# The second group's q and k as Strassen quads, v stores on GpSimd's queue, and later loads of v weights, in a fused attention and gated-MLP kernel

## The chip, the cores and the metric

One Trainium2 chip, one core. The metric is the device time of the whole kernel in microseconds (us); a version's time is the median of its runs.

## The reference: what is computed

The input x has 2048 tokens of 1024 features, in bf16. Two branches are computed from it and mixed by a gate per token:

```python
g = sigmoid((x * gate_w).sum(-1, keepdims=True))
a = A(x, wqkv, wo)       # 32 heads of 32; each token attends to 8 tokens, 2 apart, at or before it
b = B(x, w_in, w_sp, b_sp, w_out)
return g * a + (1 - g) * b
```

A is `x @ wqkv`, split into q, k and v, a softmax over the eight logits of a token and head, the weighted sum of eight v rows, and a product with `wo`. B is a gelu of `x @ w_in`, whose second half is normalised per token and mixed over all tokens with the 2048x2048 matrix `w_sp`; the product of the two halves goes through `w_out`.

## The kernel before, in words

TensorE works through these stages: a start that loads x transposed (15 transposing DMAs), makes v for the first twelve heads and q, k of group 0; then the q and k of the other seven groups of four heads, with v of the other heads and a part of z2 between; then z2, z1, the spatial product and the output product. The attention itself runs on VectorE, group after group, beside TensorE's products.

**Names.** `xT` is x transposed, tokens in the columns; `xts` holds four sums of its quarters, made by `x_sums` (line 412), eight VectorE operations of 128x2048 elements. A *tile* (`qk_tile`, line 289) is a product of q or k of one group with 512 tokens: eight matmuls of 512 columns. A *quad* is the Strassen-Winograd form of a two-by-two block product: seven products instead of eight. `qk_quad(g, c, side)` (line 895) makes q and k of group g for 1024 tokens: its first block row is q, its second is k, its block columns are tokens at 512 c and at 1024 + 512 c. It needs `xts` and four weight sums (`qk_sums`, line 881), and uses the generator `chain` (line 498), which yields after each of its seven products, of four matmuls each. Between the products lie a seed copy from bank to bank on ScalarE (L517), a copy of the shared product into SBUF on ScalarE (L523), two additions `plus` in PSUM on VectorE (L505), and four copies of the results on ScalarE (L902). One quad has four banks of its own (`bank_roles`).

**Which groups are quads.** `PAIRS = (2, 4)`: groups 2 and 3, and groups 4 and 5, are quads. Groups 0, 1, 6 and 7 are tiles. The first tile of group 1 is played at the end of the start (line 402), the other seven in the list of `group_tiles(0)` (line 943). `play_group` (line 928) plays the quads: one among the matmuls of a group's bands (`among_bands`), two interleaved.

**Bands and attention.** Logits come as bands: `band_blocks` (line 337) multiplies q and k of a group for blocks of tokens into banks 4 to 7 (L355), ScalarE casts them to fp16 (L360, L363), and they are stored to `band_d`. From there `load_bands` (line 649) gathers each token's eight logits into `att_L`. On VectorE follow maxima (L670 to L673), on ScalarE the exponential (L661), on VectorE the sum, the reciprocal and the weights (L682 to L691), and the products with v and their sums (L707, L711, L712, L716). v goes through `v_d` in DRAM too. `vp_tile` (line 298) makes v of 128 tokens for the first three groups and the gate's logit; after every fourth tile three stores of 128 KB go out (line 310), 12 in all. `load_v` (line 636) reads a group's v back, 960 KB. v of the other five groups comes from eight `v_quad`s (line 598), played in group 2, with weights `wvr` (two loads of 640 KB) and four sums of them, `wvs`.

**What sets the order.** In the start each engine's instructions stand as they are written. From line 1000 a planner runs while the program is written: it keeps a clock for each engine, one for the DMA queue, and lists of what is due (`dma`, `fill`, and three streams of attention work: maxima, weights, products). After each product of TensorE, `step` calls `advance`, which places on VectorE, ScalarE and SyncE whatever the clocks say is ready by then. The order so found is fixed in the program: an engine whose next instruction waits does nothing else. The planner starts with figures for its clocks and for the bands and v (`T_START`, line 860, and line 1007). Nearly all DMAs are issued from SyncE's queue, in that order.

**Around the change, in time.** The start ends with v tiles 12 to 15 (39.3 to 43.4 us), the first tile of group 1, and the gate: a small matmul (L405), a tanh (L406), two VectorE operations, and the stores of g and 1 - g to DRAM. Behind these in the queue are the gather of group 0's bands, the load of g as attention reads it, the load of group 0's v, group 3's weights, and group 1's v. Then the seven tiles, and from 57.5 the first quad of group 2, with group 1's bands between its products.

Of the kernel before, what the change touches and what calls it, by code (L numbers as in the profile page):

```python
# [58 lines left out]
def kernel(  # L59
# [104 lines left out]
    def load_wqk(g, dma):  # L164
        for t in range(2):
            dma(wqk_slots[g][:, t], wq_v[:, :, t * D + g * C:t * D + (g + 1) * C])
# [118 lines left out]
    def low_bank():  # L285
        half_bank[0] += 1
        return banks[half_bank[0] % 4]
# [10 lines left out]
    def vp_tile(i, bank=None, middle=None):  # L298
        ps = bank() if bank else banks[i % 2]
        for kt in range(KT):  # L300
            if kt == (2 if i else 6) and middle is not None:
                middle()
            nc.tensor.matmul(ps[:, 0:VP + 1], xT[:, kt, i * P:(i + 1) * P], wvp[:, kt, :], start=(kt == 0), stop=(kt == KT - 1))  # L303
        st = vp_slots[i // 4]
        nc.scalar.copy(st[:, i % 4, :].rearrange("p (g d h) -> p g d h", g=GP, h=HG), ps[:, 0:VP].rearrange("p (g h d) -> p g d h", g=GP, h=HG))
        nc.scalar.copy(gl_s[:, i:i + 1], ps[:, VP:VP + 1])
        if i % 4 == 3:
            for g in range(GP):
                dv = bass.AP(tensor=v_d.tensor, offset=v_d.offset + (g * (S + 16) + 16 + (i - 3) * P) * C, ap=[[C, P], [P * C, 4], [1, C]])
                sync.dma_start(dv, st[:, :, g * C:(g + 1) * C])  # L310

    warm = reg(XS_OFF, 512)
    nc.vector.memset(warm, 0.0)
# [66 lines left out]
    def first_bands(c):  # L380
        band_blocks(0, *((0, 8, 2), (1, 1, 6, 3), (4, 1, 4, 2), (6, 1, 4, 2))[c])

    for c in range(4):
        tiles = range(4 * c, 4 * c + 4) if c else ()
        for n, i in enumerate(tiles if c < 3 else ()):
            vp_tile(i, low_bank)
            if n == 0:
                first_bands(c - 1)
        if c == 1:
            for m in range(2):  # L390
                sync.dma_start(wvr[m], wq_v[:, :, 2 * D + VP + VH * m:2 * D + VP + VH * (m + 1)])
        if c == 2:
            load_wqk(2, sync.dma_start)
        for t in range(2):
            qk_tile(0, t, c)
            if c == 3 and t == 0:
                first_bands(2)
    for i in tiles:
        vp_tile(i, low_bank)
        if i == 12:  # L400
            first_bands(3)
    qk_tile(1, 0, 0)

    glT = low_bank()[0:16, 0:P]
    gate_mm = nc.tensor.matmul(glT, gl_s[:], ident32[:], start=True, stop=True)  # L405
    gate_act = nc.scalar.activation(omg[:], glT, ACT.Tanh, scale=0.5)  # L406
    nc.vector.tensor_scalar(g_s[:], omg[:], 0.5, 0.5, ALU.mult, ALU.add)
    gate_vec = nc.vector.tensor_scalar(omg_h[:], omg[:], -0.5, 0.5, ALU.mult, ALU.add)
    sync.dma_start(bass.AP(tensor=g_d.tensor, offset=g_d.offset, ap=[[P, 16], [1, P]]), g_s[:])
    gate_dma = sync.dma_start(bass.AP(tensor=og_d.tensor, offset=og_d.offset, ap=[[P, 16], [1, P]]), omg_h[:])  # L410

    def x_sums(r):
        for c in range(2):
            lo, hi = slice(512 * c, 512 * c + 512), slice(1024 + 512 * c, 1536 + 512 * c)
            a, b = ((xT[:, 0:4, hi], xT[:, 0:4, lo]), (xT[:, 4:8, hi], xts[0][:, :, lo]),
                    (xT[:, 4:8, hi], xT[:, 0:4, hi]), (xT[:, 4:8, lo], xts[1][:, :, lo]))[r]
            nc.vector.tensor_tensor(xts[r][:, :, lo], a, b, ALU.subtract)  # L417

    for r in range(4):
        x_sums(r)  # L420

    quad = [0]
    bank_roles = [banks[0:4], banks[4:8]]
# [74 lines left out]
    def chain(A11, A12, A22, S1, S2, S3, S4, B11, B21, B22, T1, T2, T3, T4, vs, put, share, N, flip=False, side=None, lean=False, done=None):  # L498

        def pairs(a, b):  # L500
            return list(zip(b, a)) if flip else list(zip(a, b))

        def plus(out, a):
            dve(N / 960.0 + 0.14, clock["PE"] + 0.2)
            last_add[0] = nc.vector.tensor_tensor(out[:, n], a[:, n], vs, ALU.add)  # L505
            return last_add[0]

        side = quad[0] % 2 if side is None else side
        X, Y, Z, V = bank_roles[side]
        bank_roles[side] = [X, V, Y, Z] if lean else [Y, V, X, Z]  # L510
        quad[0] += 1
        n = slice(0, N)
        dur, copy = N / 600.0 + 0.01, N / 1400.0 + 0.22
        pe(dur)
        product(X, pairs(A11, B11), True, N)
        act(copy, clock["PE"] + 0.2)
        last_seed[0] = nc.scalar.copy(Y[:, n], X[:, n])  # L517
        yield
        pe(dur)
        product(V, pairs(S1, T1), True, N)  # L520
        (act if share == nc.scalar.copy else dve)(copy, clock["PE"] + 0.2)
        with tc.high_priority():
            share(vs, V[:, n])  # L523
        yield
        pe(dur)
        product(Y, pairs(S2, T2), False, N)
        with tc.high_priority():
            plus(Z, Y)
        yield
        pe(dur)  # L530
        product(X, pairs(A12, B21), False, N)
        with tc.high_priority():
            put(0, 0, X)
        yield
        pe(dur)
        product(Y, pairs(S3, T3), False, N)
        if not lean:
            act(copy, clock["PE"] + 0.2)
            seed = nc.scalar.copy(X[:, n], Y[:, n])
        with tc.high_priority():  # L540
            inst = plus(V, Y)
            if not lean:
                tc.add_manual_dep(inst.ins, seed.ins.name, SYNC, reason="one reader of a bank at a time")
            put(1, 1, V)
        yield
        pe(dur)
        product(Z, pairs(S4, B22), False, N)
        with tc.high_priority():
            put(0, 1, Z)
        yield  # L550
        pe(dur)
        W = Y if lean else X
        product(W, pairs(A22, T4), False, N)
        with tc.high_priority():
            put(1, 0, W)
        if done is not None:
            done()
        yield
# [298 lines left out]
    SQH = 8  # L857
    squares = [(n, x) for n in range(16) for x in range(2)]
    LEAN = (True, True)
    T_START = (0.5, 0.0, 2.5)  # L860

    def square(n, x, junk):
        c = slice(x * HF, (x + 1) * HF)
# [4 lines left out]
            junk = junk[:, c]  # L868
        return nc.scalar.activation(junk, src, ACT.Square, accum_out=(s2, s2h)[x][:, n:n + 1])  # L869

    sums4(wvs, wvr[0][:, 0:4], wvr[0][:, 4:8], wvr[1][:, 0:4], wvr[1][:, 4:8])

    NQ = (0, 0, 0, 0, 0, 0, 0, 0)
    quads = [(0, i) for i in range(7)] + [(1, i) for i in range(8)]

    QSET = [g + x for g in PAIRS for x in range(2)]
    qs_slots = [z2h[:, 0:16, 256 + 896 * r:384 + 896 * r].rearrange("p (q k) c -> p q k c", q=4) for r in range(2)]
    qv_slots = [reg(R_OFF + 34752 + 1024 * r, 1024).bitcast(F32) for r in range(2)]
    q_landed, q_free = {}, [int(2 in PAIRS), 0]

    def qk_sums(g):
        w, s = wqk_slots[g], qs_slots[g % 2]
# [43 lines left out]
        next(quad, 0)  # L926

    def play_group(g):
        if g + 1 in PAIRS:
            among_bands(g, qk_quad(g + 1, 0, 0))  # L930
            first = qk_quad(g + 1, 1, 0)
            for _ in range(2):
                next(first)
                step()
            mark(bank_roles[1][1:3], 512)
            run(qk_quad(g + 2, 0, 1), first, step=step)
        elif g in PAIRS:
            among_bands(g, qk_quad(g + 1, 1, 0))
        else:
            return False  # L940
        return True

    def group_tiles(g):
        if g + 1 < NG:
            tiles = [lambda t=t, c=c: qk_tile(g + 1, t, c) for t in range(2) for c in range(4)][not g:]
        else:
            tiles = [lambda a=a, m=m: z2_tile(7, a, m) for m in range(2) for a in range(2)]
        if g == 0:
            return tiles

        def band(x):
            band_set(g, x)
            if x == 2:
                bands_have[0] = g + 1
        band = [lambda x=x, f=band: f(x) for x in range(3)]
        if g - 1 in PAIRS:
            return tiles[0:2] + [tiles[2], band[0], tiles[3], band[1], tiles[4], tiles[5], band[2]] + tiles[6:]
        if g + 1 < NG:
            return [tiles[0], band[0], tiles[1], band[1], tiles[2], tiles[3], band[2]] + tiles[4:]
        return [tiles[0], band[1], tiles[1], band[0], tiles[2], band[2], tiles[3]]  # L960
# [36 lines left out]
    def load_wqk_later(g, at):  # L997
        dma(at, 2.9, lambda: load_wqk(g, sync.dma_start), (lambda t: qk_ready(g, t)) if g in QSET else None)

    settle()  # L1000
    live[0] = True
    for inst in (gate_mm, gate_act, gate_vec, gate_dma):
# [1 line left out]
    for x in clock:  # L1004
        clock[x] = 0.0
    band_data[0], band_free[0], v_data[0] = T_START
    clock["SP"], clock["DMA"] = 5.5, 5.5
    stored.clear()
    bands_have[0] = 1
    next_bands()  # L1010
    dma(0.0, 0.1, lambda: sync.dma_start(g_att[:], bass.AP(tensor=g_d.tensor, offset=g_d.offset, ap=[[NJ, P], [1, NJ]])))
    next_v(1)
    load_wqk_later(3, 0.0)
    next_v()
    if 2 in PAIRS:
        fill.extend((1.5, 0.34, f) for f in qk_sums(2))
    for g in range(NG):
# [634 lines left out]
```

## Time and profile before

| | us |
|---|---|
| median of 5 runs | 653.93 |
| lowest, highest run | 652.51, 655.25 |
| the profiled execution | 654.89 |
| its span (first to last instruction) | 653.1 |
| TensorE busy in the span | 643.7 |
| VectorE busy | 515.3 |
| ScalarE busy | 295.2 |
| GpSimd (POOL) busy, 15 instructions | 6.2 |

The profile is one execution. Its page has the busy time of each engine (PE is TensorE's matmuls, PEld its weight loads, DVE VectorE, ACT ScalarE, POOL GpSimd, SP SyncE; SPq is SyncE's DMA queue), the span in 40 slices, the DMA queues, the chain that ended last, and the costliest groups of instructions. Beside the page the trace answers questions: who waited for whom, and the instructions of one engine in order of time. There a row is the start in us, the time from the start of the first to the end of the last instruction of a run of like ones, engine, line, operation, tiles and shapes, the count, and in brackets the idle time before it and who ended it. The durations of like instructions next to each other overlap a little, and a matmul's end is modelled, so starts are a better measure than ends.

The sixteen DMA engines are most busy in the start (0.85 to 1.19 of their time by tens of us from 0 to 50, where over one means that packets overlap). The granted TensorE clock is 1.00 in every slice that was asked for, from 0 to 653 us.

### The profile page before, as it was taken

To read this page: it belongs to the slowest core of one execution; us is meant where nothing else is said; L and a number is where in the kernel's file an instruction comes from. 1 tells how busy PE (TensorE), PEld (TensorE's weight loads), DVE (VectorE), ACT (ScalarE), POOL (GpSimd) and SP (SyncE) were. 2 spreads that over 40 slices of the span, in tenths; PEclk is the share of its full clock that TensorE was granted. 3 is DMA by queue.
4 is the path that set the end of the run, shared out by engine and by line. 5 is a ranking of instruction groups with operands and counts; after the bars stand their busy time and mean duration, and the time that the engine had idled before them with its cause. 6 is when DMAs were issued, how large, how long until landed. Compare 5 with 4: busy or idle time off the path is not lost.

```text
span 653.1 us, 11331 instructions
## 1 busy us (share of the span) xinstructions
PE 643.7 (99%) x4399; PEld 337.2 (52%) x4399; DVE 515.3 (79%) x808; ACT 295.2 (45%) x640; POOL 6.2 (1%) x15
## 2 busy tenths in 40 slices
PE   8999999999999999999999999999999999999998
PEld 4544467544445555444444444444444444868684
DVE  0434989999799999999988676987659999686862
ACT  3445677766677777799644112111121112202020
POOL 1000000000000000001000000000000000000000
PEclk9999999999999999999999999999999999999999
DMA  9998755697768103247995577559487364555501
GB/s 196 188 220 208 151 115 145 145 233 177 166 181 216 23 6 121 64 129 198 290 222 189 108 172 176 130 167 282 117 184 169 97 136 107 121 137 124 119 31 52
DMA packets 232934, 98.19 MB, mean 150 GB/s; under 512 B 180640, under 2 KB 220208, under 8 KB 232880
## 3 DMA queue, kind: packets, MB, share of 16 engines
q1 hardware_dynamic: 232592, 97.27, 61.5%
q8 instruction: 34, 0.56, 0.4%
q10 hardware_dynamic: 288, 0.20, 0.1%
q14 instruction: 20, 0.16, 0.1%
HBM read 44.31 MB, written 36.61 MB: 124 GB/s over the span
## 4 chain that ended last, share of the span: by engine, by line
PE 75%; DVE 8%; ACT 6%; SPq 5%; DMA 4%; issue 2%; DVEq 0%; ACTq 0%
PE psum_all L434 58%; PE psum_all L1476 8%; PE psum_all L293 5%; SPq L194 3%; PE psum_all L303 2%; ACT arena L869 2%; SPq L189 2%; ACT arena L1167 1%; DVE psum_all L505 1%; DMA band_d<-arena 1%; DVE arena L707 1%; DMA arena<-in_A_wqkv_dram 1%; PE psum_all L355 1%; SPq L178 1%; DMA arena<-in_B_w_sp_dram 1%
## 5 line engine op out<-in xcount | busy, mean ns | idle before, releaser
L434 PE MATMUL psum_all<-arena 128*128 128x512 f16 (+6 forms) x2462 | 493.3, 362 | 3.0 <-ACT psum_all L517 1.4
L434 PEld LDWEIGHTS <-arena 128*128 128x128 f16 (+1 forms) x2462 | 239.7, 98 | 249.1 <-issue 5.3
L707 DVE TENSOR_TENSOR arena<-arena,att_A 128x2048 f16<-128x2048 bf16 x64 | 75.3, 1218 | 0.3
L293 PE MATMUL psum_all<-arena 128*128 128x512 bf16 x256 | 57.5, 379 | 0.2 <-DMA arena<-in_A_wqkv_dram 0.2
L505 DVE TENSOR_TENSOR psum_all<-psum_all,arena 128x512 f32<-128x512 f32 (+1 forms) x74 | 48.2, 667 | 7.4 <-PE psum_all L434 3.7
L1476 PE MATMUL psum_all<-arena 128*128 128x256 f16 (+1 forms) x468 | 52.0, 273 | 0.2 <-ACT psum_all L1482 0.2
L1476 PEld LDWEIGHTS <-arena 128*128 128x128 f16 x468 | 45.8, 98 | 6.1 <-issue 0.3
L814 ACT ACTIVATE arena<-psum_all 128x448 bf16<-128x448 f32 x64 | 34.2, 545 | 19.3 <-PE psum_all L434 9.0
L452 ACT COPY psum_all<-psum_all 128x512 f32<-128x512 f32 (+1 forms) x24 | 12.5, 520 | 66.9 <-PE psum_all L434 60.9
L1167 ACT ACTIVATE arena<-psum_all 128x512 bf16<-128x512 f32 x56 | 31.2, 614 | 21.1 <-DMA z_d<-arena 8.0
L293 PEld LDWEIGHTS <-arena 128*128 128x128 bf16 x256 | 24.3, 98 | 28.9 <-DMA arena<-in_A_wqkv_dram 0.6
L711 DVE TENSOR_TENSOR arena<-arena 128x2048 f16<-128x2048 f16 x32 | 38.0, 1217 | 0.0
L363 ACT CAST arena<-psum_all 128x1988 f16<-128x1988 f32 (+3 forms) x25 | 34.0, 1359 | 2.4 <-PE psum_all L355 2.0
L296 ACT CAST arena<-psum_all 128x512 bf16<-128x512 f32 x32 | 18.6, 585 | 27.2 <-PE psum_all L293 27.2
L869 ACT ACTIVATE arena<-arena 128x896 bf16<-128x896 bf16 x32 | 30.9, 980 | 0.0
L476 ACT COPY psum_all<-psum_all 128x512 f32<-128x512 f32 (+1 forms) x24 | 12.3, 518 | 37.5 <-PE psum_all L434 36.8
L576 DVE TENSOR_TENSOR arena<-arena 128x512 f16<-128x512 bf16 (+3 forms) x52 | 25.4, 521 | 2.3 <-DMA arena<-in_A_wqkv_dram 1.9
L417 DVE TENSOR_TENSOR arena<-arena 128x2048 f16<-128x2048 bf16 x8 | 9.4, 1222 | 20.1 <-DMA arena<-in_A_x_dram 20.0
L580 DVE TENSOR_TENSOR arena<-arena 128x1024 f16<-128x1024 f16 (+2 forms) x17 | 12.1, 719 | 15.7 <-PE psum_all L434 15.7
L458 ACT COPY arena<-psum_all 128x512 f32<-128x512 f32 (+1 forms) x24 | 12.7, 533 | 26.0 <-PE psum_all L434 22.5
L463 ACT COPY psum_all<-psum_all 128x512 f32<-128x512 f32 (+1 forms) x24 | 12.4, 516 | 25.6 <-PE psum_all L434 24.8
L303 PE MATMUL psum_all<-arena 128*128 128x385 bf16 x128 | 22.7, 328 | 0.9 <-DMA arena<-in_A_x_dram 0.5
(112 smaller groups left out, 523.7 us busy)
## 6 DMA issues: line engine op xcount, KB each, us to landing
arena<-v_d SPq DMA_DIRECT2D x8, 960.0 KB, 7.5
z_d<-arena SPq DMA_DIRECT2D x14, 512.0 KB, 4.8
arena<-z_d SPq DMA_DIRECT2D x14, 512.0 KB, 4.2
zg_d<-arena SPq DMA_DIRECT2D x56, 128.0 KB, 2.2
arena<-zg_d SPq DMA_DIRECT2D x32, 224.0 KB, 3.1
band_d<-arena SPq DMA_DIRECT2D x28, 248.5 KB, 4.7
arena<-in_A_wqkv_dram SPq DMA_DIRECT2D x16, 256.0 KB, 4.2
o_d<-arena SPq DMA_DIRECT2D x4, 1024.0 KB, 6.0
```

The costliest lines, as they stand in the source:

```text
L293: nc.tensor.matmul(ps[:], w[:, t, kt, :], xT[:, kt, 512 * c:512 * (c + 1)], start=(kt == 0), stop=(kt == KT - 1))
L303: nc.tensor.matmul(ps[:, 0:VP + 1], xT[:, kt, i * P:(i + 1) * P], wvp[:, kt, :], start=(kt == 0), stop=(kt == KT - 1))
L363: nc.scalar.copy(dst, src)
L434: nc.tensor.matmul(bank[:, 0:N], lhsT, rhs, start=(start and m == 0), stop=(m == n - 1), skip_group_check=True)
L505: last_add[0] = nc.vector.tensor_tensor(out[:, n], a[:, n], vs, ALU.add)
L576: return [lambda a=a: nc.vector.tensor_tensor(*a) for a in args]
L707: lambda ws=ws, in0=in0, in1=in1: tt(p5[:, ws], in0[:, ws], in1[:, ws], ALU.mult)), False
L711: lambda a=p3[:, ws], b=p3[:, ws.start + 4:ws.stop + 4]: tt(a, a, b, ALU.add)), not n
L814: nc.scalar.activation(z2[:, i + 8 * a, ZC * c:ZC * (c + 1)], bank[:, 0:ZC], ACT.Gelu_apprx_tanh, accum_out=s1[:, 4 * n + c:4 * n + c + 1])
L869: return nc.scalar.activation(junk, src, ACT.Square, accum_out=(s2, s2h)[x][:, n:n + 1])
L1167: last_gelu[0] = nc.scalar.activation(z1s[:, f, a, :], bank[:], ACT.Gelu_apprx_tanh)
L1476: nc.tensor.matmul(bank[:, h], l, r, start=(start and m == 0), stop=(m == len(ab) - 1), skip_group_check=True)
```

## The change

Five edits belong together:

- **q and k of group 1 are two quads** instead of eight tiles. Their weight sums are made at the end of the start; the x sums are made in the start in the order of the tokens that they need (`x_sums(0)` behind v tiles 8 to 11, `x_sums(1)` one stage later). The first two products of the first quad come before the gate's matmul, where the first tile was; the other products, and then the second quad, make `play_group(0)`, one after the other, not interleaved. The last start stage uses banks that the quad doesn't need first.
- **The twelve stores of the first groups' v** (line 310) are issued by GpSimd's queue instead of SyncE's.
- **The v weights of the later groups** (`wvr`) are no longer loaded in the start, but by the planner behind the gather of group 0's bands, the load of g and the load of group 0's v; their four sums become work for the planner (`fill`) instead of standing ahead of the gate on VectorE.
- **The planner's first figures** change: `T_START` from (0.5, 0.0, 2.5) to zeros, the clocks of SyncE and the DMA from 5.5 to 0.5 and 1.5.
- **Bookkeeping** that follows: `q_free` starts with both slots taken, and `chain` counts a quad only where no side is given.

```diff
             for g in range(GP):
                 dv = bass.AP(tensor=v_d.tensor, offset=v_d.offset + (g * (S + 16) + 16 + (i - 3) * P) * C, ap=[[C, P], [P * C, 4], [1, C]])
-                sync.dma_start(dv, st[:, :, g * C:(g + 1) * C])
+                (nc.gpsimd if i < 16 else sync).dma_start(dv, st[:, :, g * C:(g + 1) * C])
...
-        if c == 1:
-            for m in range(2):
-                sync.dma_start(wvr[m], wq_v[:, :, 2 * D + VP + VH * m:2 * D + VP + VH * (m + 1)])
+        if c > 1:
+            x_sums(c - 2)
         if c == 2:
             load_wqk(2, sync.dma_start)
         for t in range(2):
-            qk_tile(0, t, c)
+            qk_tile(0, t, c, (lambda: banks[1 + t]) if c == 3 else low_bank)
...
     for i in tiles:
-        vp_tile(i, low_bank)
+        vp_tile(i, lambda: banks[3 * (i % 2)])
         if i == 12:
             first_bands(3)
-    qk_tile(1, 0, 0)
+    for f in qk_sums(1):
+        f()
+
+    first_quad = qk_quad(1, 0, 0)
+    for _ in range(2):
+        next(first_quad)
...
-    T_START = (0.5, 0.0, 2.5)
+    T_START = (0.0, 0.0, 0.0)
...
-    sums4(wvs, wvr[0][:, 0:4], wvr[0][:, 4:8], wvr[1][:, 0:4], wvr[1][:, 4:8])
...
     def play_group(g):
-        if g + 1 in PAIRS:
+        if g == 0:
+            run(first_quad, step=step)
+            run(qk_quad(1, 1, 0), step=step)
+        elif g + 1 in PAIRS:
...
-    clock["SP"], clock["DMA"] = 5.5, 5.5
+    clock["SP"], clock["DMA"] = 0.5, 1.5
...
     next_v(1)
+    def load_wvr():
+        for m in range(2):
+            sync.dma_start(wvr[m], wq_v[:, :, 2 * D + VP + VH * m:2 * D + VP + VH * (m + 1)])
+
+    dma(0.0, 3.7, load_wvr, lambda t: fill.extend((t + LATE, 0.75, f) for f in sums4_steps(wvs, wvr[0][:, 0:4], wvr[0][:, 4:8], wvr[1][:, 0:4], wvr[1][:, 4:8])))
     load_wqk_later(3, 0.0)
     next_v()
```

## The prediction

> **What bounds the kernel now.** I read the page's first part, then TensorE's waits, then the order of time of TensorE, ScalarE, VectorE and the SyncE queue around 45 to 90 us, where the change acts. The page's head:
>
> ```profile
> span 653.1 us, 11331 instructions
> ...
> PE 643.7 (99%) x4399; PEld 337.2 (52%) x4399; DVE 515.3 (79%) x808; ACT 295.2 (45%) x640; POOL 6.2 (1%) x15
> ```
>
> TensorE is idle for 653.1 - 643.7 = 9.4 us in all. About 2.4 us of it lie before 12 us and 3.1 us behind the last matmul, which ends at 650.0. So a change pays if it takes matmuls away, or one of the few stalls between. Those are, with total, count and longest:
>
> ```profile
> PE psum_all L434 <- ACT psum_all L517: 1.4, 2, 1.2
> ...
> PE psum_all L355 <- ACT arena L363: 0.8, 2, 0.6
> PE psum_all L434 <- ACT arena L902: 0.7, 1, 0.7
> ```
>
> The longest comes at 60.8, in the first Strassen quad of group 2. TensorE and then ScalarE, in order of time:
>
> ```profile
> 45.36 12.26 PE L293 MATMUL psum_all<-arena 128*128 128x512 bf16 x56
> ...
> 58.62 1.04 PE L434 MATMUL psum_all<-arena 128*128 128x512 f16 x4
> 60.82 1.02 PE L434 MATMUL psum_all<-arena 128*128 128x512 f16 x4 [1.16 <-ACT psum_all L517]
> ```
> ```profile
> 59.65 0.63 ACT L661 ACTIVATE att_L<-att_L 128x512 f16<-128x512 f16 x1 [1.41 <-DVE att_L L673]
> 60.19 0.58 ACT L517 COPY psum_all<-psum_all 128x512 f32<-128x512 f32 x1
> ```
>
> The seed copy L517 stands behind the first exponential L661, which waits for VectorE's maxima, which wait for the gather of bands. VectorE and the queue show why that is late:
>
> ```profile
> 58.38 0.29 DVE L670 TENSOR_TENSOR att_m<-att_L 128x256 f16<-128x256 f16 x1 [8.09 <-DMA att_L<-band_d]
> ```
> ```profile
> 45.53 6.21 SPq L189 DMA_DIRECT2D band_d<-arena  x8
> 51.84 1.73 SPq L189 DMA_DIRECT2D v_d<-arena  x3
> 53.67 0.47 SPq L189 DMA_DIRECT2D g_d<-g_s  x1
> 54.24 0.36 SPq L189 DMA_DIRECT2D og_d<-omg_h  x1
> 54.70 1.28 SPq L189 DMA_DIRECT2D att_L<-band_d  x2
> ```
>
> The queue is solid from 45.5 on, with stores whose data were ready at 37 to 44.
>
> **Part 1, fewer matmuls.** The eight q/k tiles of group 1 are 8 x 8 = 64 matmuls of 512 columns; two quads are 2 x 7 x 4 = 56. The row at 45.36 gives 12.26 / 56 = 0.219 us each, the steady steps of the chain 1.73 / 8 = 0.216. Removed: 8 x 0.216 = 1.73 us, all on TensorE's path. No other matmul is added; the built program has 16 TensorE rows fewer, eight loads and eight products.
>
> The quads add work beside it. Four weight sums of 128x512 (1.56 us for four, L576) wait for group 1's weights, issued at 27.7 and landed by about 33; with the eight sums of x, which run at 24.8 to 34.7 already and only change order, they are done near 37, against a first use at 43.4: nothing. If that cover went, 1.56 us. Four VectorE additions into PSUM (0.70 each, L505) and four ScalarE copies (0.58) stand between the products. One product takes 4 x 0.216 = 0.865 us and covers one copy or one addition if the engine is free. I walked it from 43.4, where the first product now starts. In the first quad the second addition stands behind three weight sums of group 2 (1.2 us), ends at 48.95 and holds the last product back 0.1 us. In the second quad the first addition stands behind the four maxima (1.24 us), which wait for the gather: it is free if that lands by about 51.2. Both quads end at about 55.9 instead of 57.5: -1.73 + 0.11 = -1.62.
>
> **Part 2, the queue.** Taken off SyncE ahead of the gather: twelve v stores, of which only the last three (1.73) stand in the rows above, and two v-weight loads. The band stores now go out as soon as their casts end: the last four at 40.7 to 43. g_d then waits for the gate alone (about 46.2, as TensorE reaches it two products behind the v tiles). From g_d's start to the landing was 58.3 - 53.67 = 4.6 us, so the gather lands at 46.3 + 4.6 = 50.9, and the exponential starts at 52.3, 7.4 us earlier, ahead of group 2's seed copy by 4 us. The 1.16 us stall goes. By the starts of the matmuls it costs 60.82 - (58.62 + 0.865) = 1.33, since the product's tail no longer overlaps: -1.33. What is late next is VectorE (part 3).
>
> **The POOL queue.** Stores of 128 KB in 512 rows of 256 bytes. No row shows a DMA from POOL. Lower bound per store: the 0.58 us that SyncE takes (1.73 / 3). For the upper, the Trainium skill's page SBUF — State Buffer (section "SBUF: two separate sides", with its subsection on the bandwidth pool) speaks against the change: GpSimd writes such descriptors itself and is locked out while VectorE runs certain instructions; a DMA of about 0.62 us became 3.1 us. The row: VectorE is busy at 24.8 to 34.7 with two-input operations, over the third batch (due at 30.9), and has only short ones at 44 to 50, over the last. By the page the third batch could take 9.3 us and end at 40; by the SyncE row it ends at 32.7. Either leaves it before the last batch at 44. I take 1.3 per store, nearer the SyncE row, for the last batch lies in a quiet VectorE. Group 0's last store then lands at 44 + 1.3 + 2.4 (landing of v_d rows) = 47.7, before SyncE reaches the first v load at 49.2; at 3.1 it lands at 49.5, 0.3 late. The first batch moves from 30.5 to 12.4, into the loads of x. Three stores alone filled the DMA engines for about 2.3 us; the tiles of x had 1 to 2 us between landing and use. Between 0 and 1 us of TensorE wait; I take 0.2. It cannot be a gain.
>
> **Part 3, what moves onto VectorE.** Four sums of the v weights (0.82 each, 3.3 us) ran at 43 to 46 on an idle VectorE. Now they stand among attention work and the additions of group 2's first quad. Two waits are new there. The v weights are issued behind the first v load, at 49.8; v load and weights are 0.98 + 1.31 MB, and the DMA moved 292 to 354 GB/s at 58 to 66, so at 250 to 300 they land at 58.5 to 60. Queued behind these sums is the quad's second addition, and TensorE's seventh product waits for it; it hides the sums up to a landing at 60.1, beyond which each us is one for TensorE. I take no stall. Then VectorE is continuously busy to about 82.5, when group 3's second addition ends (85.4 before). From 54.9 that is 27.6 us against 23.3 before: the sums, plus one product (1.2) now ahead of group 1's maxima. Before, TensorE's v quads started 2.9 us behind that addition, because the bank they need is read by a copy that stands behind the cast L363. So they start at 82.5 + 2.9 = 85.4 against 88.33, while TensorE alone would have been ready for them a little sooner: the stall there grows by about 0.3. From there on the orders of VectorE, ScalarE and SyncE are as before, so the shift is kept to the end. If a transfer is late, this chain gives it all back.
>
> **Sum.** -1.62 - 1.33 + 0.2 + 0.3 = -2.45; I say -2.4. The profiled execution took 654.89 (span 653.1 and 1.8 around it), so it would take 652.5. It lies 0.96 above the median of 653.93; the predicted median is 651.5.
>
> **Rivals.** About 0.3%, 2.0 us, is what a measurement can tell from no change, so the forecast stands just beyond it.
> (a) As above: 651.5.
> (b) VectorE becomes the bound of 55 to 88. For it: no gap in my walk, and the v weights land within half a us of their need. Against: VectorE was still idle 0.9 us in that stretch before. One or two us late at the sums or the gather, one for one: -2.4 + 1.4 = -1.0, 652.9.
> (c) The stalls at 84 to 88 vanish too, because VectorE is early: -1.73 - 1.33 - 0.8 = -3.9, 650.1. Against it is the longer VectorE list.
> (d) Slower: descriptors on POOL. Twelve stores go out in order, from 12.4; the batches come at 12.4, 21.7, 30.9 and 44. Up to 3.8 us a store the backlog is gone by about the last batch. Beyond it the tenth store, on which the first v load waits, ends at 12.4 + 10 t: at t = 4.5 it lands at 59.8, 10 us late, of which 2 are slack: -2.4 + 8 = +5.6, 659.5. It beats the rest from t = 4.1. Against it: 0.58 on SyncE and the page's 3.1 in the worst case.
> (e) The early stores don't bring the gather forward, because TensorE's gate sets g_d: then only part 1 acts, -1.6, 652.3. The gate is at 45 in either kernel, so I count this with (b).
>
> **How the numbers follow.** (a) 0.48, (b) with (e) 0.28, (c) 0.08, (d) 0.16. The range takes (a) to (c) with their spread: 650.0 to 655.0. Faster by over 0.3% (below 651.97): three quarters of (a), nearly all of (c), a little of (b): 0.50. Within 0.3%: 0.34. Slower: 0.16.
>
> **What would show it.** Eight fewer 512-column products and two quads at 43 to 56; band gather landing near 51; no wait of a seed copy behind the first exponential near 57; v-weight sums near 60 without an addition waiting behind them; v quads from about 85.4; POOL stores 1 to 3 us apart. The prediction is wrong if POOL's stores come more than 3.8 us apart, if the v weights land behind 60, or if x lands late before 21 us.

## The result, and the profile after

The changed kernel takes 651.03 us (median), against 653.00 for the kernel before in runs on the same chip: a ratio of 0.997, with a 95% interval of 0.9959 to 0.998, so 2.0 us less (1.3 to 2.7). The profiled execution has a span of 649.2 us, in one of 651.03. The head of the page after:

```profile
span 649.2 us, 11344 instructions
...
PE 641.9 (99%) x4391; PEld 336.8 (52%) x4391; DVE 519.2 (80%) x816; ACT 297.7 (46%) x644; POOL 15.4 (2%) x27
```

TensorE has eight matmuls and 1.8 us of busy time less, VectorE 3.9 us more, and GpSimd 9.2 us more, which are the twelve stores. TensorE's waits in total, count and longest:

```profile
...
PE psum_all L355 <- ACT arena L363: 0.8, 2, 0.6
PE psum_all L402 <- DVE psum_all L473: 0.5, 1, 0.5
PE psum_all L402 <- ACT arena L869: 0.4, 1, 0.4
...
```

The quads' lines have moved: a product is L402 here (L434 before), an addition L473 (L505), the seed copy L486 (L517), the copy of a result L869 (L902), the first maximum L639 (L670), the exponential L630 (L661). The wait for a seed copy, 1.2 us before, is gone from 60 us. TensorE in order of time, after and then before where its v quads start:

```profile
42.60 1.89 PE L402 MATMUL psum_all<-arena 128*128 128x512 bf16 x8
...
44.75 11.83 PE L402 MATMUL psum_all<-arena 128*128 128x512 f16 x52
...
56.71 1.90 PE L402 MATMUL psum_all<-arena 128*128 128x512 f16 x8
...
84.88 0.70 PE L402 MATMUL psum_all<-arena 128*128 128x320 f16 x4 [0.44 <-ACT arena L869]
```
```profile
88.33 0.70 PE L434 MATMUL psum_all<-arena 128*128 128x320 f16 x4 [0.66 <-ACT arena L902]
```

The rows at 42.60 and 44.75 are the two quads and the first product of group 2's first quad. No row up to 60 us in this view has a bracket, yet 52 matmuls take 11.83 us, 0.227 each, where the 56 of before took 12.26, 0.219 each: very short waits are there that the list of waits doesn't show. The row at 56.71 is where before stood still. The queue and VectorE:

```profile
36.04 8.08 SPq L189 DMA_DIRECT2D band_d<-arena  x12
45.88 0.35 SPq L189 DMA_DIRECT2D g_d<-g_s  x1
...
46.79 1.28 SPq L189 DMA_DIRECT2D att_L<-band_d  x2
...
48.98 0.35 SPq L189 DMA_DIRECT2D arena<-v_d  x1
49.38 6.72 SPq L189 DMA_DIRECT2D arena<-in_A_wqkv_dram  x4
```
```profile
50.49 0.29 DVE L639 TENSOR_TENSOR att_m<-att_L 128x256 f16<-128x256 f16 x1 [1.83 <-DMA att_L<-band_d]
...
59.33 1.68 DVE L545 TENSOR_TENSOR arena<-arena 128x1280 f16<-128x1280 bf16 x2
61.06 0.70 DVE L473 TENSOR_TENSOR psum_all<-psum_all,arena 128x512 f32<-128x512 f32 x1
...
81.30 0.70 DVE L473 TENSOR_TENSOR psum_all<-psum_all,arena 128x512 f32<-128x512 f32 x1 [0.35 <-PE psum_all L402]
```

The band stores end at 44.1, so the gate now sets the store of g. The gather lands at 50.49, 7.9 us earlier than before; the sums of the v weights at 59.33 do not wait for their load, and the addition behind them comes at 61.06. GpSimd's stores:

```profile
12.14 2.43 POOL L310 DMA_DIRECT2D v_d<-arena  x3 [9.46 <-ACT gl_s L306]
...
30.69 2.23 POOL L310 DMA_DIRECT2D v_d<-arena  x3 [7.07 <-ACT gl_s L306]
43.58 2.23 POOL L310 DMA_DIRECT2D v_d<-arena  x3 [10.65 <-ACT gl_s L306]
```

A store takes 2.23 / 3 = 0.74 us of GpSimd in the batches at 21.4 (not shown), 30.7 and 43.6, and 2.43 / 3 = 0.81 in the first.

**Where the time came from.** The two profiles, of before and of after, differ by 3.9 us, more than the medians do: the execution of before lay 1.9 us above the median of 653.00. So both kernels were run again, and all versions are read by stages. A is the first product behind the last v tile, B the first product of group 2's first quad, C the second product of the first v quad (where 0.44 us was waited above), D the end of the last matmul. "Gather" is the start of the first maximum, as far as it waited for the landing. All in us; the ratio is to before on the same chip. The stages are those of one execution each, the ratio is that of the medians.

| kernel | A | gather - A | B - A | C - A | D - C | ratio and interval |
|---|---|---|---|---|---|---|
| before | 43.22 | 15.16 | 14.24 | 45.11 | 561.70 | |
| before, again | 42.62 | 14.46 | 14.24 | 44.40 | 560.95 | 0.9997 [0.9989, 1.0005] |
| after | 42.60 | 7.89 | 12.95 | 42.27 | 560.86 | 0.997 [0.9959, 0.998] |
| after, again | 43.05 | 8.06 | 12.94 | 42.27 | 559.91 | 0.9958 [0.9943, 0.9974] |
| quads alone | 42.77 | 14.64 | 14.53 | 43.86 | 562.70 | 1.0029 [1.0022, 1.0037] |
| queue alone | 42.76 | 7.90 | 14.24 | 43.79 | 560.29 | 1.0001 [0.999, 1.0012] |
| all stores on SyncE | 42.58 | 11.04 | 17.21 | 46.53 | 559.99 | 1.0038 [1.0025, 1.0051] |
| first nine on SyncE | 42.79 | 11.64 | 17.41 | 46.73 | 562.97 | 1.0009 [0.9992, 1.0027] |
| last three on SyncE | 42.58 | 8.36 | 12.94 | 42.27 | 560.06 | 0.9983 [0.9973, 0.9994] |
| v weights in the start | 42.72 | 11.79 | 18.76 | 48.74 | 562.59 | 1.0088 [1.0067, 1.0108] |
| stores twice | 43.68 | 12.64 | 19.61 | 49.29 | 560.76 | 1.003 [1.0016, 1.0044] |
| sums early | 42.43 | 7.96 | 12.94 | 42.27 | 560.52 | 0.9957 [0.9943, 0.9971] |
| maxima behind | 42.91 | (no wait) | 12.94 | 42.43 | 563.14 | 1.0019 [1.0007, 1.0032] |
| maxima behind, stores on SyncE | 42.66 | 15.81 | 12.95 | 45.22 | 563.23 | 1.0061 [1.0039, 1.0084] |

A is the same in both kernels (the 0.6 us between the two shown profiles is chance), so nothing was lost in the start. From "before, again" to after, B - A falls by 1.29 and C - B by 0.84, together 2.13 us, about what the medians show. A single execution need not be typical, though: the one in "before, again" lay 0.9 us above the median of its kernel, those in "first nine on SyncE" and "stores twice" 3.5 and 3.3 us above, and the one in "last three on SyncE" was the fastest of ten.

### The profile page after: what moved, and what is told of

Its sections match the earlier page's. It is cut to its first block, busy times and chain, and to the rows that moved or that the text cites. A ratio compares the mean times of both kernels' runs of the same rounds, so it can differ in the third digit from the quotient of the medians.

```text
span 649.2 us, 11344 instructions
## 1 busy us (share of the span) xinstructions
PE 641.9 (99%) x4391; PEld 336.8 (52%) x4391; DVE 519.2 (80%) x816; ACT 297.7 (46%) x644; POOL 15.4 (2%) x27
## 4 chain that ended last, share of the span: by engine, by line
PE 87%; DVE 4%; ACT 4%; DMA 2%; SPq 1%; issue 1%; DVEq 0%
PE psum_all L402 71%; PE psum_all L1484 8%; PE psum_all L293 4%; PE psum_all L303 2%; ACT arena L838 2%; DVE arena L676 1%; PE psum_all L355 1%; DMA band_d<-arena 1%; ACT arena L1175 1%; DVE arena L680 1%; DVE psum_all L473 1%; SPq L178 1%; DVE arena L545 1%; DMA arena<-in_A_wqkv_dram 1%; ACT arena L783 0%
## 5 line engine op out<-in xcount | busy, mean ns | idle before, releaser
L402 PE MATMUL psum_all<-arena 128*128 128x512 f16 (+6 forms) x2518 | 505.7, 362 | 1.5 <-DVE psum_all L473 0.5
L402 PEld LDWEIGHTS <-arena 128*128 128x128 f16 (+1 forms) x2518 | 245.2, 98 | 254.1 <-issue 4.4
L473 DVE TENSOR_TENSOR psum_all<-psum_all,arena 128x512 f32<-128x512 f32 (+1 forms) x78 | 51.0, 669 | 8.9 <-PE psum_all L402 5.8
L293 PE MATMUL psum_all<-arena 128*128 128x512 bf16 x192 | 43.3, 380 | 0.1
L420 ACT COPY psum_all<-psum_all 128x512 f32<-128x512 f32 (+1 forms) x24 | 12.5, 520 | 65.8 <-PE psum_all L402 60.5
L545 DVE TENSOR_TENSOR arena<-arena 128x512 f16<-128x512 bf16 (+5 forms) x60 | 30.0, 534 | 0.4
L444 ACT COPY psum_all<-psum_all 128x512 f32<-128x512 f32 (+1 forms) x24 | 12.3, 518 | 37.5 <-PE psum_all L402 36.8
L293 PEld LDWEIGHTS <-arena 128*128 128x128 bf16 x192 | 18.1, 98 | 21.4 <-DMA arena<-in_A_wqkv_dram 0.5
L869 ACT CAST arena<-psum_all 128x512 bf16<-128x512 f32 x40 | 22.2, 592 | 12.5 <-DVE psum_all L473 9.8
L486 ACT COPY psum_all<-psum_all 128x512 f32<-128x512 f32 (+1 forms) x39 | 21.8, 572 | 6.2 <-PE psum_all L402 5.5
L431 ACT COPY psum_all<-psum_all 128x512 f32<-128x512 f32 (+1 forms) x24 | 12.4, 516 | 25.6 <-PE psum_all L402 23.7
L549 DVE TENSOR_TENSOR arena<-arena 128x1024 f16<-128x1024 f16 (+1 forms) x16 | 11.3, 713 | 15.7 <-PE psum_all L402 15.7
```

The lines of the kernel that those rows point to most:

```text
L293: nc.tensor.matmul(ps[:], w[:, t, kt, :], xT[:, kt, 512 * c:512 * (c + 1)], start=(kt == 0), stop=(kt == KT - 1))
L402: nc.tensor.matmul(bank[:, 0:N], lhsT, rhs, start=(start and m == 0), stop=(m == n - 1), skip_group_check=True)
L545: return [lambda a=a: nc.vector.tensor_tensor(*a) for a in args]
L869: nc.scalar.copy((qT_slots, kT_slots)[t][g % 2][:, :, 256 * (c + 2 * x):256 * (c + 2 * x + 1)], bank[:].rearrange("p (n e) -> p e n", e=2))
```

## The experiments

The theory: the quads save eight matmuls but place their additions on VectorE behind maxima that wait for the gather; the queue edits bring the gather forward, and each part is worth little without the other. The rival: the parts add up, each with its own gain, and GpSimd's queue and the place of the v weights don't matter by themselves.

### Both kernels again

Nothing is edited.

> The kernel before, unchanged, profiled a second time. By all theories its time is that of before (ratio 1.000 within 0.002). It tells what of the 3.9 us between the two profiled spans is chance. My theory: the 1.16 us wait of the seed copy behind the first exponential near 60 us is there again, and the first v quad starts 2.3 to 3.0 us later than in the changed kernel, counted from the first product behind the v tiles. Rival (only eight matmuls count, the rest is one slow execution): the wait near 60 us is much smaller or gone in this second profile, and the difference is about 1.3 us.

> The changed kernel, unchanged, timed and profiled again beside the other three. Ratio to before 0.997 within 0.0015. In its profile the v quads start about 42.3 us behind the first product behind the v tiles, if the gather and the v weights land as they did; if one lands later by more than 0.5 us the time follows it.

Ratios of 0.9997 and 0.9958. In this second profile of before, the wait that the prediction began from is this:

```profile
58.02 1.04 PE L434 MATMUL psum_all<-arena 128*128 128x512 f16 x4
59.51 1.02 PE L434 MATMUL psum_all<-arena 128*128 128x512 f16 x4 [0.45 <-ACT psum_all L517]
```

It is 0.45 us, where the first profile had 1.16. By starts it costs 59.51 - (58.02 + 0.865) = 0.62, where the first had 1.33. The gather came 0.7 us earlier behind A, and the wait shrank by as much. A stall at the end of a chain of transfers is not a constant of the kernel; one profile gives one draw of it.

### One part alone

The queue edits without the quads:

```diff
-        if g == 0:
-            run(first_quad, step=step)
-            run(qk_quad(1, 1, 0), step=step)
-        elif g + 1 in PAIRS:
+        if g + 1 in PAIRS:
...
-    first_quad = qk_quad(1, 0, 0)
-    for _ in range(2):
-        next(first_quad)
...
+    qk_tile(1, 0, 0)
...
```

> The changed kernel with group 1 as eight tiles again: the queue part of the change alone. My theory: the seed copy's wait is gone, worth 1.3 us against before, and the eight matmuls are back; but here three of the four v-weight sums stand ahead of the first addition of group 2's quad, and the weights land near 59, so that up to 1.3 us of it may return: 0 to 1.3 us faster than before. Rival (only the matmuls count): as before within 0.3 us with no wait of the seed copy moved. Rival (the queue is all): 2 us faster than before, the same as the whole change.

And the quads with the stores on SyncE, the v weights in the start and the planner's old figures:

```diff
-                (nc.gpsimd if i < 16 else sync).dma_start(dv, st[:, :, g * C:(g + 1) * C])
+                sync.dma_start(dv, st[:, :, g * C:(g + 1) * C])
...
-    T_START = (0.0, 0.0, 0.0)
+    T_START = (0.5, 0.0, 2.5)
...
+    sums4(wvs, wvr[0][:, 0:4], wvr[0][:, 4:8], wvr[1][:, 0:4], wvr[1][:, 4:8])
...
```

> Group 1 as quads with everything else of the queue as before: v stores on SyncE, v weights loaded and summed in the start, the planner's old first figures, by which it puts group 0's maxima behind the four additions of the two quads. My theory, after the first four runs: the quads alone shorten TensorE's list by 1.3 us net, but the attention's gather comes as late as before (about 57), and VectorE's list from there to the last addition ahead of the v quads is as long as before, so that the v quads start at most 0.6 us earlier than before, counted from the first product behind the v tiles: 0 to 0.6 us faster than before. Rival (the two parts simply add): 1.3 us faster than before.

The queue alone: the gather is as early as in after, the seed copy's wait is gone and C - B falls by 0.61, exactly its cost; but a time of 1.0001 (0.999 to 1.0012) shows no gain, and 0.6 us would lie at the edge of that interval. The quads alone make the kernel slower, by 0.3% (0.22 to 0.37). Its first quad shows why, TensorE and then VectorE:

```profile
47.36 1.89 PE L402 MATMUL psum_all<-arena 128*128 128x512 f16 x8 [0.55 <-DVE psum_all L473]
50.15 8.18 PE L402 MATMUL psum_all<-arena 128*128 128x512 f16 x35 [0.90 <-DVE psum_all L473]
```
```profile
45.62 0.83 DVE L552 TENSOR_TENSOR arena<-arena 128x1280 f16<-128x1280 bf16 x1
...
48.26 1.22 DVE L545 TENSOR_TENSOR arena<-arena 128x512 f16<-128x512 bf16 x3 [0.95 <-DMA arena<-in_A_wqkv_dram]
49.40 0.69 DVE L473 TENSOR_TENSOR psum_all<-psum_all,arena 128x512 f32<-128x512 f32 x1
```

The v-weight sums, in the start again, run until 46.4, and the addition behind them is late. Then group 2's sums wait for weights that the old queue brings late, and the next addition is behind them. So B - A is 0.29 us longer than with tiles, and the 1.73 us of the eight matmuls are spent already. Another 1.9 us are waited at 299 us, where the planner placed a block of attention products ahead of an addition ("maxima behind" below has the same wait).

By the medians the parts do not add up: about 0 and +0.3% make -0.3%. But +0.3% is 1.9 us, as much as the wait at 299 us, which belongs to the planner's order there and not to the quads. Without it the parts would make about 0, where both together make 2.0 us. Up to C the picture is less sharp: the quads alone gain 0.54 us, the queue alone 0.61, both 2.13 by "before, again", an excess of 1.0; by the first profile of before it is 0.3. So simple addition does not fit, but how large the excess is stays open. This pair also doesn't test the maxima, for with the planner's old figures they stand behind the quads' additions in "quads alone"; the next runs do.

### The queue part taken apart

All twelve stores back on SyncE (`sync.dma_start` for all i), all else as after:

> The changed kernel, but with the twelve v stores of the first groups on SyncE's queue again. My theory: the queue has room for them once the early loads are gone. Counting 0.6 us per issue from 30.4 us on, the last three stores end at about 46.6 and the gate's store starts 0.7 us later than in the changed kernel (45.9), so that the bands are gathered at about 51.2 instead of 50.5, still in time for the first addition of the second quad: no change in time, within 0.4 us of the changed kernel. Rival (the move to GpSimd's queue brings the gain): the gather lands 2 us or more later, the additions of the second quad wait behind the maxima, and 1 us or more of the gain is lost.

Only the last three on SyncE (`i < 12` in place of `i < 16`):

> The changed kernel with only the last batch of v stores (three of twelve) on SyncE again. In the changed kernel SyncE has nothing to issue between the last band store (44.1) and the gate's store (45.9): 1.8 us, and three issues take 1.7. My theory (what counts is when the gather is issued): it moves by 0 to 0.4 us, and the time is that of the changed kernel within 0.4 us. Rival (the last batch on SyncE is what made the run with all stores on SyncE slow): 1.5 to 3 us slower than the changed kernel.

Only the first nine on SyncE (`i > 12`):

> The kernel after, with the first nine v stores on SyncE and only the last three on GpSimd (the opposite of the run that moved only the last three). My theory: on SyncE the bands of the last tokens go out behind the nine stores and behind the other start loads, so the store of g comes at 46.5 to 48 and the gather lands at 51.5 to 53; the point where that starts to cost is about 51.2. So TensorE waits 0.3 to 1.8 us for an addition in the second quad of group 1[...]: from the first product behind the v tiles to the second product of the first v quad 42.6 to 44.1 us instead of 42.27, and a time 0.3 to 1.8 us above after's. Rival (only all twelve stores together fill the queue; nine early ones lie in its gaps): the store of g at 46.3, 42.27 us, the time of after.

The v weights loaded and summed in the start as before, the stores on GpSimd:

> The changed kernel, but with the two v-weight loads in the start and their four sums on VectorE ahead of the gate, as before; stores stay on GpSimd's queue. My theory: the queue has room, the gather lands at most 0.7 us later, and VectorE has 3.3 us less between 55 and 82 us, so the additions there end earlier and the wait in front of the first v quad (0.4 us at 84.9) shrinks: 0 to 0.6 us faster than the changed kernel. Rival (these loads are what kept the queue busy): the gather lands 2 us or more later and the time goes back by 1 us or more.

My expectation for the twelve stores fell: I had 51.2 for the landing and the store of g not later. It went out at 48.79, the gather landed at 53.62, and TensorE waited 2.66 us in the second quad:

```profile
44.73 8.13 PE L402 MATMUL psum_all<-arena 128*128 128x512 f16 x36
55.52 5.30 PE L402 MATMUL psum_all<-arena 128*128 128x512 f16 x16 [2.66 <-DVE psum_all L473]
60.75 0.27 PE L355 MATMUL psum_all<-arena 32*64 32x64 bf16 x16
```
```profile
48.79 0.48 SPq L189 DMA_DIRECT2D g_d<-g_s  x1
```
```profile
53.62 0.29 DVE L639 TENSOR_TENSOR att_m<-att_L 128x256 f16<-128x256 f16 x1 [4.98 <-DMA att_L<-band_d]
...
54.77 0.69 DVE L473 TENSOR_TENSOR psum_all<-psum_all,arena 128x512 f32<-128x512 f32 x1
```

This is the coupling: the addition at 54.77 stands behind the four maxima, and the product behind it starts 0.06 us after it ends. The last three stores alone do nothing to the stages of the execution that was profiled (42.27): they fill a gap in the queue between 42.8 and the gate. Yet the median with them lies 1.1 us above that of after on the same chip (651.42 and 650.33; the intervals of the two ratios just touch), where I had expected 0.4 at most. The profiled execution was the fastest of its ten, and by the line below it met the condition by 0.02 us only, so slower ones may miss it; no profile shows one. The first nine cost more, for they stand ahead of the bands: the last eight band stores go out from 42.74 on, behind the third batch, and end at 49.2. I had expected 0.3 to 1.8 us from them; by the stages it was 4.46, by the ratio's distance to after's about 3. The stages show a late execution: 7 of the 22 had a mean clock of 0.997 or less, as it had, and 15 had 1.00. For the v weights in the start I had expected a gain of 0 to 0.6 us over after. They cost the most, about 8 us by the ratio's distance to after's: a wait of 3.41 us in this place, and 1.67 more near 197 us.

One line holds for all four kernels in which the gather was late for the addition. Where the maxima stand ahead of the addition, TensorE's wait is the landing behind A less 8.38 us: 11.04 - 8.38 = 2.66 fixes it, and it gives 3.26, 3.41 and 4.26 for first nine, v weights and stores twice, which measured 3.27, 3.41 and 4.27. After lands at 7.89 and 8.06, so its margin is 0.3 to 0.5 us; with the last three stores on SyncE, which landed at 8.36, it was 0.02.

### GpSimd's queue, priced

Each store is issued twice, the second into a scratch tile in DRAM:

```diff
+                d2 = bass.AP(tensor=v2_d.tensor, offset=v2_d.offset + (g * (S + 16) + 16 + (i - 3) * P) * C, ap=[[C, P], [P * C, 4], [1, C]])
+                nc.gpsimd.dma_start(d2, st[:, :, g * C:(g + 1) * C])
```

> The kernel after, with each of the twelve v stores issued by GpSimd twice, the second time into a scratch tile in DRAM that nobody reads. It prices GpSimd's queue, the slower rival of the forecast. My theory: a store takes 0.74 us of GpSimd, so three pairs take about 4.5 us instead of 2.2, and the last batch ends at about 48.1 in place of 45.8. The load of v on SyncE waits for the last store of its group to land, 4.1 us behind its issue: until about 52 in place of 50, so the v load and the v weights behind it come 1 to 2.5 us later, and the v-weight sums, which did not wait at 59.3, wait 0 to 1 us for them; TensorE 0 to 1 us. The time is 0 to 1 us above after's. The rival (descriptors on GpSimd slow[...]): a doubled backlog at 24 to 38 us shows up as stores that come over 1.5 us apart, the last at over 52 us, and the time rises by over 3 us.

GpSimd took 0.75 us for each of the 24 but the first (0.92), and issued the last at 48.4, so the rival's mechanism isn't there. But the time rose by more than I said (1.003 against after's 0.997). SyncE's queue in the profiled execution, a slow one, tells why: the last x transposes were issued until 32.02 (29.00 in after), the twelve band stores took 10.39 us (8.08), the store of g came at 50.18 (45.88), and TensorE waited 4.27 us for the addition. So more traffic in the start delays SyncE's transfers even when another queue issues it, and GpSimd's time is no limit. The queue counts too: "first nine on SyncE" moves the same bytes as after.

### VectorE's list and its order

Group 2's weight sums made in the start, so that VectorE has less to do at 46 to 49 (`for f in qk_sums(1) + qk_sums(2)`):

> The changed kernel with the four weight sums of group 2 (0.4 us each) made in the start on an idle VectorE, instead of between the additions of group 1's first quad. My theory: the two waits of 0.09 us in the first quad go, VectorE's list from 46 to 82 us is 1.6 us shorter, and the wait in front of the first v quad (0.44 us) shrinks: 0.1 to 0.5 us faster than the changed kernel, the v quads 0.2 to 0.5 us earlier counted from the first product behind the v tiles. Rival (VectorE does not bound that stretch, ScalarE's casts do): no change.

The same, with the planner's figure for the bands at 2.0, which places the maxima behind all four additions of the quads (`T_START = (2.0, 0.0, 0.0)`):

> The kernel after, with group 2's weight sums already in the start and the planner's first figure for the bands at 2.0, which places group 0's maxima behind the four additions of both quads on VectorE. My theory: group 1's quads then do not depend on the gather at all; since it lands at 50.2 in after anyway, the quads end as before (first product of group 2's first quad 12.94 us behind the first product behind the v tiles, at best 0.1 less), and the attention of group 0 starts up to 2 us later, which VectorE makes good by 82 since its list is no longer. From the first product to the second of the first v quad 42.0 to 42.6 us; the time within 0.5 us of after's. Rival (VectorE's list bounds 50 to 82): each us that the maxima start later shows again at the v quads, 43 to 44 us, and the time is 1 to 2 us above after's.

And that with all v stores on SyncE:

> The kernel with group 0's maxima behind all four additions of the two quads on VectorE, and all twelve v stores back on SyncE. It takes away the one place where the quads wait for the gather and leaves the late gather. My theory: the gather lands as late as with the stores on SyncE in the kernel after (11 us behind the first product behind the v tiles, where 8.4 us was the point beyond which TensorE waited), but TensorE waits for no addition: from the first product to group 2's first quad 12.9 to 13.1 us instead of 17.21, and no drop of the clock. Attention starts 3 us later, so VectorE is later at the v quads by 0 to 1.5 us: 42.4 to 44 us to the second product of the first v quad, against 46.53 with the order of after. The time is that of the kernel with the maxima behind, 0 to 1.5 us above. Rival (a late queue costs the same wherever the maxima stand, since the v load and the v weights come late too): group 2's first quad or the sums behind it wait instead, 46 us or more to the v quads, and a time 4 us above.

With the sums early no stage moves, where I had expected 0.1 to 0.5 us: VectorE's list between 46 and 49 is not what holds the quads. With the maxima behind, C - A is 42.43, as I expected, but the time is not: 1.0019 where after has about 0.997. The loss lies far from the edit:

```profile
298.35 1.89 PE L402 MATMUL psum_all<-arena 128*128 128x512 f16 x8 [1.84 <-DVE psum_all L473]
```

Another first figure gave the planner another order at 290 us, with the additions of a quad of that stage behind a block of attention products. So it is no version that beats after.

With the late gather too, B - A stays at 12.95 where the order of after had 17.21. That shows the coupling by itself: without the maxima ahead of the addition, the quads don't care when the gather lands. It landed 15.81 us behind A and not the 11 that I expected. The store of g went out later (50.65, where "all stores on SyncE" had 48.79), and the planner's figure of 2.0, as in "maxima behind", also put the gather behind the loads of g and of v in SyncE's queue: it was issued at 53.32, there at 49.82. And 2.8 us are lost a stage later, where I had 0 to 1.5. TensorE, then ScalarE:

```profile
61.26 0.64 PE L355 MATMUL psum_all<-arena 32*64 32x71 bf16 x56 [2.59 <-ACT arena L363]
```
```profile
59.74 0.63 ACT L630 ACTIVATE att_L<-att_L 128x512 f16<-128x512 f16 x1 [2.44 <-DVE att_L L642]
...
60.62 0.59 ACT L363 CAST arena<-psum_all 128x512 f16<-128x512 f32 x1
```

The gather landed at 58.5, and this is the stall of the kernel before in another place: the first exponential waits at the head of ScalarE's list, and a cast that TensorE needs stands behind it. There are two such places, an addition behind the maxima and a copy behind the exponential, and an early gather clears both.

## Why the prediction was right, step by step

It gave -2.4 us; the medians show -2.0 and the stages -2.13. Direction and mechanism were right, and four sizes were off, which partly cancel.

- **"Removed: 8 x 0.216 = 1.73 us".** Eight matmuls fewer, and nothing else added on TensorE.
- **"Holds the last product back 0.1 us" (+0.11).** Too small: 0.44 us (1.73 less the 1.29 by which B - A fell). Four products start 0.09 to 0.16 us late, together 0.43. I took it that a product of 0.865 us covers an addition of 0.70; with the hand-over from TensorE to VectorE and back the product behind comes 0.865 + 0.09 = 0.955 after the one that is covered, and once 0.07 later still. Nothing else holds them: the waits are the same with the sums early.
- **"The 1.16 us stall goes ... -1.33".** It went, by the steps named: the store of g at 45.9 (46.2 said), the gather at 50.5 (50.9), the exponential at 51.77 (52.3). The size came from one profile; the second has 0.62, and the queue alone takes 0.61 off it. This is the term that was off most, by 0.7.
- **The POOL queue.** "I take 1.3 per store": 0.74. The lower end was nearer. The lock-out doesn't show: the third batch ran beside VectorE's sums of x and took 2.23 us like the last, beside a quieter VectorE. It should not have been expected either, for the prediction read the Trainium skill's page SBUF — State Buffer wrongly. The section "Who interferes with whom" says that `tensor_tensor`, which all sums of x are, has no two-port mode and was not seen to stall a DMA. So the 9.3 us for the third batch didn't follow from it, and the case that it describes was not tested here. "I take 0.2" for the late x: the transposes did come later (the load of group 1's weights, issued behind the last of them, came at 29.05 and not 27.70), but A didn't move: 0.
- **"I take no stall" at the v-weight sums.** Right: 59.33 without a wait.
- **"The stall there grows by about 0.3".** It shrank by 0.22, from 0.66 to 0.44. The chain was right, an addition's end plus 2.9: 82.0 + 2.9 = 84.9. VectorE was done at 82.0 and not 82.5. The product counted on top (1.2) had only changed its place, six of them lie in the stretch in both kernels, and VectorE's busy time in it grew by 25.43 - 22.15 = 3.28, the sums alone. Nor was it continuously busy: ahead of the additions at 58.7, 67.4 and 81.3 it waits for TensorE, 0.3 to 0.5 us each. These two errors cancel in part, which is luck.

-2.45 + 0.33 + 0.71 - 0.2 - 0.52 = -2.13.

The rivals: (d) needed more than 4.1 us a store and is out. (b), VectorE as the bound, is out, since VectorE itself waits for TensorE three times in that stretch. (c) is there in part, 0.2 of 0.8. Of (e) the premise holds, the gate does set the store of g, yet the gather gains 7.9 us.

What the prediction lacked: it put the parts in a sum, though it said itself that the second quad is free only if the gather lands by about 51.2. That condition was the larger matter. After meets it by 0.3 to 0.5 us. Where it was missed by 2.66 to 4.27 us, B came 4.27 to 6.67 us later, since TensorE's clock fell as well. A rival "gather at 53, 4 us slower" was missing.

**What stays open.** In two of the runs with a late gather (first nine, v weights in the start) TensorE waits another 1.7 to 2.1 us for an addition near 196 us, with the instructions in the order of after; in the two others with that order it doesn't, or for 0.2. Why wasn't settled. Nor was it whether the slower executions with the last three stores on SyncE wait for the gather. Beyond C, D - C varies by 1 us between runs of one kernel.

## What to carry to other kernels

An edit that puts new work on an in-order engine inherits every wait that stands ahead of that work: ask what the instruction in front waits for, when that lands, and how far it may slip before the critical engine notices. Edits that are each worth nothing alone can be worth something together, so undo them one at a time before crediting one, and look in each such run for losses far from the edit that another order brings. And take the size of a stall from two profiles where the sum rests on it.

## What the runs showed of the hardware

**A wait can halve TensorE's clock for what follows.** With all stores on SyncE, by stretches, the granted clock is the column behind POOL's:

```profile
50.00:55.00 5.00, 2.85 (x14) 1.16 (x12) 1.28 (x5) 1.28 (x4) 0.00 (x0) 1.00 0.69 164
55.00:60.00 5.00, 4.48 (x13) 1.69 (x13) 3.71 (x10) 2.17 (x5) 0.00 (x0) 0.66 1.04 333
60.00:65.00 5.00, 5.00 (x92) 2.37 (x91) 3.65 (x5) 3.93 (x6) 0.00 (x0) 1.00 1.15 326
```

The 16 matmuls behind the wait took 5.30 us: by starts 60.75 - 55.52 = 5.23, which is 1.77 more than 16 x 0.216 = 3.46, on top of the wait of 2.66. Their starts are 0.427 us apart from 56.1 to 59.1, then 0.216 again.

The Trainium skill, page TensorE: Matmul & The Clock Gate (Part 1, the HAM clock gate), has the half rate, after an idle window of about 3.4 us, and windows that run free of the program. The half rate and the windows agree: in the record of the granted clock that each of the fourteen traces has, every change lies a whole multiple of 3.413 us behind the first one on record, and in the four executions where the gather was late for the addition the clock was at half for one such window (3.41 us: all stores on SyncE, first nine) or two (6.83: v weights in the start, stores twice). In the last three of these it fell 0.8 to 1.0 us before the wait was over. But a window need not be idle throughout. With matmuls counted as 0.216 us from their start, windows in which TensorE stood still for 2.65 (first nine), 2.70 (v weights), 2.83 (all stores) and 3.39 us (stores twice) brought the drop. No window at full clock up to 330 us with 2.01 us or less did. The gap of 2.75 us at 58.5 in the last experiment lay across two windows, 1.0 us in one and 1.8 in the other, and the clock stayed. By these rows it depends on where the window stands whether a wait of some 2.7 us halves the clock too. Of 17 executions with all stores on SyncE 11 had a mean clock of 0.997 or less, and 6 had 1.00; how long those six waited is not on record.

**GpSimd issued a 128 KB store of 512 rows of 256 bytes in 0.74 us** (0.81 in the first batch), beside VectorE's two-input sums as beside a quieter VectorE, against 1.73 / 3 = 0.58 on SyncE; it landed 4.1 us after its issue, against 2.4 from SyncE (medians of the twelve). The records count 576 packets for the twelve, against 6,336 fewer on SyncE's queue, for the same bytes.
